# An mLSTM cell and a squared-ReLU FFN on one core: two block sums, two products and one rounding step change their places

## The chip, the cores and the metric

The kernel runs on one core of a Trainium2 chip. The metric is the device time of one execution in microseconds, as the median of several runs. A core has TensorE (PE, matmuls and their weight loads), VectorE (DVE), ScalarE (ACT), GpSimd (POOL) and SyncE (SP, whose queue issues nearly all DMAs here). Each engine takes its own instructions in the order in which they were written, and waits for the others by semaphores.

## The reference

Two layers follow each other. The first is an mLSTM cell, a recurrence over 768 steps for 4 x 8 heads of 40 elements, with a gated state; the second an FFN without bias on its 3072 output rows of 8 x 40 = 320 elements.

```python
batch, n_heads, seq, head_dim = (4, 8, 768, 40)
for t in range(S):
    m_new = np.maximum(f_gate[:, :, t] + m, i_gate[:, :, t])
    f_stab = np.exp(f_gate[:, :, t] + m - m_new)
    i_stab = np.exp(i_gate[:, :, t] - m_new)
    m = m_new
    C = f_stab[..., None, None] * C + i_stab[..., None, None] * np.einsum('bhd,bhe->bhde', vt, kt)
    n = f_stab[:, :, None] * n + i_stab[:, :, None] * kt
    h_tilde = np.einsum('bhde,bhe->bhd', C, qt)
    denom = np.maximum(np.abs(np.einsum('bhd,bhd->bh', n, qt)[:, :, None]), 1.0)
    y[:, :, t] = 1.0 / (1.0 + np.exp(-o_gate[:, :, t])) * h_tilde / denom
# rows (b, t), columns (head, d): x is 3072 x 320, w_in 320 x 2048, w_out 2048 x 320
h = np.maximum(x @ w_in, 0.0)
out = h * h @ w_out
```

The weights come as 64-bit floats and are rounded to 32 bits on the chip.

## The kernel before

**Chunks and groups.** The sequence is cut into chunks of 128 steps, six for each batch element, 24 in all (s = 0 to 23). Within a chunk the recurrence is a causal matrix of 128 x 128 for each head: the scores k q (`scores`, L415, into `tp`) are multiplied on DVE by weights W made on ACT (L384), which gives P (`weighted`, L435). From chunk to chunk the state C is handed on. Two chunks make a group of 256 rows for the FFN, 12 groups in all (g = 0 to 11).

**A chunk in its later form (s from 6 on).** `score(s)` puts the scores on PE and P on DVE, and for chunks that do not begin a sequence also the scaled query, `scale_q` (L483, written as `kq` over a buffer of that name). `attend_turned(s)` (L493) puts the numerator on PE, first from the state and the scaled query (L505), then from the values and P (L512), then the state's increment dC (L522); DVE turns the numerator (L527, `tn`) and adds up the state (L533). The numerator goes to memory and back in another order (`move_num`); `normalise_turned` (L553 to L562) makes x of it on DVE; `store_rows` sends x to memory and brings it back in squares, which `turn_squares` transposes on DVE (L597, `xT`) one chunk later. `turn_kq` (L315) is the same for k and q of a chunk to come.

**The FFN of a group.** `ffn1_main` and `ffn1_rest` (L621, L632) are x times w_in, in four parts; ACT takes the relu (L647, `r_sb`) and DVE squares it (L654) into `g2`. From group 1 on, the second product is the fast one of `ffn2_fast`: a product of 2 x 2 blocks by seven products in place of eight (each `product`, L715, is eight matmuls of eight block columns). It needs sums of blocks of the weights (T0, T1, T2, and one written over a part of `w_out`; `sums_of_weights`, L689 to L696) and of the activations (S1, S2, the third written into `g2` itself, and S4; `sums`, L710, one DVE instruction each of 128 x 1024 elements). It runs in four steps with two banks X and Y in PSUM:

- step 0: X = A11 B11, copied by ACT (L735) to `m1`; Y = S2 T1, added by DVE to `m1`
- step 1: X += A12 B21, copied to the result by ACT (L740); Y += (third sum) times B12, which DVE adds up
- step 2: a product with T2 and one with T0, each added up by DVE; the upper half of the rows goes out
- step 3: the product with S4 is added to the bank that holds the one with T0, and DVE adds it up; the other half goes out

**What sets the order.** It is written out by hand. A list `parts` holds one FFN part for each place n (1: first product, 2: second); s = 6 + n // 4 is the chunk that is worked on beside it and at = n % 4 the quarter of it. The loop at L926 puts, at each place, first what belongs to at 0, 1 or 3 (the score, the numerator, the normalising), then sums, then the FFN part, then what belongs to at 2 or to the end. From n = 8 on, step 0 of a group falls on at 0 and step 1 on at 1 of a chunk with even s, step 2 and 3 on at 2 and 3 of the next one; the first product of group g + 2 stands between. While chunks last, then, one group takes two chunks.

**Weights.** `Rounding` brings the 64-bit weights in pieces (26 in all) and turns them into 32-bit ones: two ACT instructions, three DVE instructions (L206, L210, L211) and one on GpSimd (L215) for each piece. A table, NEXT, says how many pieces are done after each place.

Of the kernel before, what the change touches and what calls it, by code (L numbers as in the profile page):

```python
# [29 lines left out]
def kernel(  # L30
# [38 lines left out]
    NPAIR = NF // 2  # L69
    GT = 2  # L70
    NG = NT // GT
# [76 lines left out]
    pieces = []  # L148
# [81 lines left out]
    rounding = Rounding()  # L230
# [452 lines left out]
    T = {}  # L683
# [36 lines left out]
    def ffn2_fast(g, step):  # L720

        if step == 0:
            st["y"] = [ffn.tile([P, DM], F32, name="y_sb", bufs=3) for _ in range(2)]
        if step in (0, 2):
            st["o2"] = [ps_h.tile([P, W], F32, name="h_ps") for _ in range(2)]
        (X, Y), (y1, y0) = st["o2"], st["y"]
        g4 = st["g2", g][:].rearrange("p (f two) t -> p f two t", two=2)
        cols = [slice(n * P, (n + 1) * P) for n in range(2)]
        S1, S2, S4 = st["S"]
        X, Y = X[:, :DH], Y[:, :DH]  # L730
        add = lambda to, a, b: nc.vector.tensor_tensor(to, a, b, op=ALU.add)  # L731
        m1, u12, u22 = y1[:, :DH], y0[:, DH:], y1[:, DH:]
        if step == 0:
            product(X, g4[:, :, 0, cols[0]], B11, start=True)
            nc.scalar.copy(m1, X)  # L735
            product(Y, S2, T[1], start=True)
            add(u12, Y, m1)
        elif step == 1:
            product(X, g4[:, :, 1, cols[0]], B21)
            nc.scalar.copy(y0[:, :DH], X)  # L740
            product(Y, g4[:, :, 0, cols[1]], B12)
            add(u22, Y, m1)
        elif step == 2:
            product(Y, g4[:, :, 1, cols[1]], T[2], start=True)
            add(m1, u22, Y)
            product(X, S1, T[0], start=True)
            add(u22, u22, X)
            t = g * GT + 1
            nc.sync.dma_start(out[t * P : (t + 1) * P, :], y1[:])
        else:  # L750
            product(X, S4, B22)
            add(u12, u12, X)
            t = g * GT
            nc.sync.dma_start(out[t * P : (t + 1) * P, :], y0[:])
# [94 lines left out]
    rounding.step()  # L849


    NEXT = (5, 8, 10, 11, 13, 15, 17, 19, 21, 23, 25, 26)
    assert NEXT[-1] == len(pieces)
    for u in range(8):
        s = 2 + u // 2
        relu_half()
# [64 lines left out]
    for g in range(1, NG):  # L921
        parts += [(2, g, i) for i in range(2)]
        if g + 2 < NG:
            parts += [(1, g + 2, i) for i in range(4)]
        parts += [(2, g, i) for i in range(2, 4)]
    for n, (which, g, i) in enumerate(parts):  # L926
        s, at = 6 + n // 4, n % 4
        if n == 1:
            decays(s + 1)
            mask(s + 1)  # L930
        if n == 4:
            brought.close()
            late = ctx.enter_context(tc.tile_pool(name="late", bufs=1, side="right"))
        if at == 0:
            do(score, s)
        if at == 1:
            do(attend_turned, s)
            if s > X_SQ:
                do(turn_squares, s - 1)
        if 5 <= n < 8:  # L940
            sums_of_weights(n - 5)
        if n == 6:
            sums(1, slice(0, NPAIR), (1, 2))
        if n == 8:
            sums_of_weights(3)
            sums(1, slice(0, NPAIR), (3,))
        if n == 9:
            sums(1, slice(0, NPAIR), (4,))
        new_sums = which == 2 and 0 < g < NG - 1 and i == 3
        if new_sums:  # L950
            for one in (1, 2, 3):
                sums(g + 1, slice(0, NPAIR), (one,))
        if at == 3:
            do(normalise_turned, s)
            do(store_rows, s)
            if s % 4 == 3:
                for r in range(s + 1, min(s + 5, NT)):
                    sigmoid(r)
        if which == 1:
            ffn1_main(g, i)  # L960
            if i % 2 == 0:
                held = st["half"]
            else:

                both = held, st["half"]
                for more, half in enumerate(both):
                    ffn1_rest(g, i - 1 + more, half[0])
                for half in both:
                    st["half"] = half
                    relu_half()  # L970
                    square_half()
        elif g == 0:
            ffn2(g, *divmod(i, 2))
        else:
            ffn2_fast(g, i)
        if new_sums:
            sums(g + 1, slice(0, NPAIR), (4,))
        if at == 2:
            do(load_squares, s + 2)
            do(weigh_on, s + 1)  # L980
            do(turn_kq, s + 1)
        if at == 3:
            do(decay_C, s + 1)
        if n < 4:
            while rounding.done < NEXT[8 + n]:
                rounding.step()
        if at == 1:
            do(move_num, s)
            do(load, s + 4)
            if 8 <= s < 20:  # L990
                load_o(s + 4)
            do(pair_up, s + 3)
# [30 lines left out]
```

## Time and profile before

| | |
|---|---|
| median of 3 runs | 565.14 us (563.45 to 567.63) |
| the profiled execution | 565.71 us, its span 563.9 us |
| PE busy | 534.4 us, 95% of the span |
| DVE busy | 333.9 us, 59% |
| ACT busy | 193.1 us, 34% |
| GpSimd busy | 95.5 us, 17% |
| mean granted PE clock | 0.976 of full speed |

A timeline row has the start in us from the span's start, the length in us, the engine, the line, the operation, the tiles written and read, the shape and the count of instructions merged; in square brackets stand the idle time of the engine before it and what ended it. PEld is the weight load of a matmul, which overlaps the one before. A matmul on 32-bit floats is two passes, so eight matmuls are 16 in a row of the timeline. The ends of matmuls are modelled, so rows of PE that follow each other closely overlap by some hundredths. The span is the time from the first to the last instruction; the execution's time is 1.8 us longer.

### The profile page before, as it was taken

The numbers are of one execution on the slowest core, as the hardware profiler recorded it, in microseconds if no ns is written. First come the engines' busy times: TensorE is split into PE (matmuls) and PEld (weight loads), VectorE is DVE, ScalarE is ACT, GpSimd is POOL, SyncE is SP. The second block draws the span as 40 slices with busy tenths as digits, with TensorE's granted clock in tenths as the row PEclk, the third lists the DMA queues.
The fourth block names the chain that finished last, engine by engine and source line by source line (L and its number), as shares of the span: only waits on it lengthen the run. The fifth ranks groups of instructions, "written<-read, shape, count | busy, mean of one in ns | idle before, by whom it ended". The sixth has DMA issues, their size and how long they took to land.

```text
span 563.9 us, 10278 instructions
## 1 busy us (share of the span) xinstructions
PE 534.4 (95%) x3928; PEld 464.6 (82%) x3929; DVE 333.9 (59%) x620; ACT 193.1 (34%) x460; POOL 95.5 (17%) x110
## 2 busy tenths in 40 slices
PE   9989899997999899999899989999989989999997
PEld 5878788876888798888888878898878878898997
DVE  8588988685945833844844655565664555341540
ACT  3767577451442221532321623321523313102100
POOL 3354623231120210010310201000200201000000
PEclk9897999998999989999989989999999989999999
DMA  9988788854665764756756736657645321110000
GB/s 194 239 181 174 155 194 210 188 117 109 143 131 118 145 132 107 154 123 127 146 107 123 145 89 136 127 134 135 137 115 112 71 65 45 48 42 1 25 23 24
DMA packets 238353, 67.53 MB, mean 120 GB/s; under 512 B 185728, under 2 KB 232832, under 8 KB 238304
## 3 DMA queue, kind: packets, MB, share of 16 engines
q1 hardware_dynamic: 238208, 66.68, 55.1%
q8 instruction: 31, 0.51, 0.4%
q10 hardware_dynamic: 96, 0.20, 0.1%
q14 instruction: 18, 0.15, 0.1%
HBM read 54.56 MB, written 17.86 MB: 128 GB/s over the span
## 4 chain that ended last, share of the span: by engine, by line
PE 83%; DVE 9%; DMA 3%; ACT 2%; issue 1%; SPq 1%; POOL 0%; DVEq 0%; POOLq 0%; ACTq 0%
PE h_ps L715 30%; PE h_ps L621 27%; PE h_ps L632 7%; PE numT L512 4%; PE tp L422 4%; PE numT L505 3%; PE h_ps L661 2%; DVE P_sb L435 2%; DVE g L654 2%; PE hp L458 1%; PE dC L522 1%; DMA num_rows<-tn 1%; DVE mag L210 1%; ACT W_sb L384 1%; PE tp L410 1%
## 5 line engine op out<-in xcount | busy, mean ns | idle before, releaser
L621 PE MATMUL h_ps<-xT,w_in 128*128 128x256 f32 x768 | 175.3, 384 | 1.2 <-ACT xT L606 0.6
L621 PEld LDWEIGHTS h_ps<-xT,w_in 128*128 128x128 f32 x768 | 143.8, 191 | 23.1 <-issue 1.2
L654 DVE TENSOR_TENSOR g<-r_sb 128x512 f32<-128x512 f32 x96 | 61.7, 701 | 76.4 <-ACT r_sb L647 76.4
L647 ACT ACTIVATE r_sb<-h_ps 128x512 f32<-128x512 f32 x96 | 49.9, 601 | 152.5 <-PE h_ps L632 149.3
L715 PE MATMUL h_ps<-w_out,g 128*128 128x160 f32 x528 | 78.4, 306 | 0.0
L715 PEld LDWEIGHTS h_ps<-w_out,g 128*128 128x128 f32 x528 | 73.9, 193 | 1.4
L358 POOL TENSOR_SCALAR_AFFINE_SELECT A_bc<-A_bc 128x1024 f32<-128x1024 f32 x22 | 25.7, 1168 | 222.3 <-ACT kq L368 128.5
L384 ACT ACTIVATE W_sb<-A_bc,b_T 128x128 f32<-128x128 f32 x176 | 53.8, 392 | 24.1 <-POOL A_bc L358 24.1
L715 PE MATMUL h_ps<-T,S 128*128 128x160 f32 x352 | 51.4, 299 | 0.0
L632 PE MATMUL h_ps<-xT,w_in 64*128 64x256 f32 x384 | 49.0, 391 | 0.0
L715 PEld LDWEIGHTS h_ps<-T,S 128*128 128x128 f32 x352 | 49.0, 190 | 0.0
L632 PEld LDWEIGHTS h_ps<-xT,w_in 64*128 64x128 f32 x384 | 34.8, 186 | 12.3 <-issue 9.0
L527 DVE STREAM_TRANSPOSE tn<-numT 128x512 f32<-128x512 f32 x18 | 12.9, 717 | 41.5 <-PE numT L512 41.5
L396 POOL TENSOR_TENSOR vw<-va,W_sb 128x328 f32<-128x328 f32 x20 | 20.1, 1006 | 86.5 <-ACT W_sb L384 69.7
L505 PE MATMUL numT<-kq,C 40*64 40x128 f32 x240 | 18.5, 299 | 15.4 <-DVE kq L483 15.4
L740 ACT COPY y_sb<-h_ps 128x160 f32<-128x160 f32 x11 | 3.2, 292 | 82.9 <-PE h_ps L715 82.9
L715 PE MATMUL h_ps<-w_out,S 128*128 128x160 f32 x176 | 26.8, 306 | 4.5 <-DVE y_sb L731 4.5
L505 PEld LDWEIGHTS numT<-kq,C 40*64 40x64 f32 x240 | 14.5, 144 | 19.8 <-issue 12.6
L435 DVE TENSOR_TENSOR P_sb<-tp,W_sb 128x512 f32<-128x512 f32 x46 | 29.5, 682 | 1.9 <-PE tp L422 1.9
L715 PEld LDWEIGHTS h_ps<-w_out,S 128*128 128x128 f32 x176 | 24.2, 190 | 7.2 <-DVE y_sb L731 7.2
L731 DVE TENSOR_TENSOR y_sb<-y_sb,h_ps 128x160 f32<-128x160 f32 x33 | 10.5, 319 | 27.6 <-PE h_ps L715 26.6
L422 PEld LDWEIGHTS tp<-kqT 40*128 40x128 f32 x384 | 24.2, 187 | 3.3 <-issue 1.3
(119 smaller groups left out, 648.6 us busy)
## 6 DMA issues: line engine op xcount, KB each, us to landing
A_bc<-a_rows SPq DMA_DIRECT2D x22, 512.0 KB, 4.8
raw<-in_moe_w_out_dram SPq DMA_DIRECT2D x16, 320.0 KB, 3.3
num_rows<-tn SPq DMA_DIRECT2D x18, 256.0 KB, 2.2
kq<-num_rows SPq DMA_DIRECT2D x72, 64.0 KB, 1.9
kqT<-kq_rows SPq DMA_DIRECT2D x34, 128.0 KB, 3.0
raw<-in_moe_w_in_dram SPq DMA_DIRECT2D x8, 512.0 KB, 4.9
kq<-in_k_dram SPq DMA_DIRECT2D x24, 160.0 KB, 3.4
va<-in_v_dram SPq DMA_DIRECT2D x24, 160.0 KB, 3.8
```

Of the source, the lines that this page charges most:

```text
L358: nc.gpsimd.affine_select(A[:], A[:], compare_op=ALU.is_ge, fill=-1e30, base=0, pattern=[[0, H], [1, P]], channel_multiplier=-1,)
L384: nc.scalar.activation(d["W"][:, i * n + h, :], A[i][:, h, :], AF.Exp, bias=b_T[:, b, c, i * n + h : i * n + h + 1],)
L396: nc.gpsimd.tensor_tensor(d["vw"][:], d["va"][:], d["W"][:, :, P - 1 : P].to_broadcast([P, H, D1]), op=ALU.mult,)
L422: nc.tensor.matmul(sc[i][:, j, :], lhsT=d["kT"][rows, j, :], rhs=d["qT"][rows, j, :], start=True, stop=True,)
L435: nc.vector.tensor_tensor(t, d["sc"][i], d["W"][:, heads, :], op=ALU.mult)
L505: nc.tensor.matmul(numT[halves[i], j, :], lhsT=C[live[i], j * D1 : j * D1 + DP], rhs=d["eA"][live[i], j, :], start=(j == 0), stop=False, s ...
L512: nc.tensor.matmul(numT[halves[i], j, :], lhsT=va_w[s % NKQ][:, h * D1 : h * D1 + DP], rhs=d["P"][h % 2][:, h // 2, :] if s < KQ_SQ else d ...
L621: nc.tensor.matmul(hs[i][:, n, :], lhsT=w_in[:, a, fb * P : (fb + 1) * P], rhs=xT[:, :, a, :], start=(n == 0 and a == 0), stop=False,)
L632: nc.tensor.matmul(hs[i][:, n, :], lhsT=w_in2[rows, 2 * pp + n, :], rhs=xT[rows, :, 2, :], start=False, stop=(n == 1),)
L647: nc.scalar.activation(rs[-1][:], h[:], AF.Relu)
L654: nc.vector.tensor_tensor(g4[:, :, i, :], r[:], r[:], op=ALU.mult)
L715: nc.tensor.matmul(to, lhsT=lhsT[:, p], rhs=rhs[:, p, :], start=(start and p == 0), stop=(p == NPAIR - 1), skip_group_check=True,)
```

## The change

Three things move; no arithmetic is added or taken away.

1. The third and fourth block sum of the activations. Before, all four of group g + 1 were queued at step 3 of group g, three ahead of the normalising and the fourth behind the step's product. Now the first two stay there, the third is queued at step 0 of group g + 1 behind `score`, and the fourth at step 1 behind `attend_turned` and `turn_squares`. Group 1 is as it was.
2. The order in `ffn2_fast`. In step 2 the product with T0 (bank X) comes ahead of the one with T2 (bank Y), and the adds of steps 1 and 2 write to other halves of `y1` accordingly.
3. The last rounding step. The table's end (now LAST) has 25 at n = 3 in place of 26, and a fifth entry, so that piece 26 is rounded at the end of n = 4, behind P of chunk 7. The pool in which T0 to T2 and the sums lie, which takes the place of the rounding's buffers, is opened at n = 5 in place of n = 4.

```diff
@@ ffn2_fast @@
             product(Y, g4[:, :, 0, cols[1]], B12)
-            add(u22, Y, m1)
+            add(m1, m1, Y)
         elif step == 2:
+            product(X, S1, T[0], start=True)
+            add(u22, m1, X)
             product(Y, g4[:, :, 1, cols[1]], T[2], start=True)
-            add(m1, u22, Y)
-            product(X, S1, T[0], start=True)
-            add(u22, u22, X)
+            add(m1, m1, Y)
             t = g * GT + 1
             nc.sync.dma_start(out[t * P : (t + 1) * P, :], y1[:])
@@ the loop over parts @@
+    LAST = (21, 23, 25, 25, 26)
     for n, (which, g, i) in enumerate(parts):
...
-        if n == 4:
+        if n == 5:
             brought.close()
             late = ctx.enter_context(tc.tile_pool(name="late", bufs=1, side="right"))
...
-        new_sums = which == 2 and 0 < g < NG - 1 and i == 3
-        if new_sums:
-            for one in (1, 2, 3):
+        if which == 2 and 0 < g < NG - 1 and i == 3:
+            for one in (1, 2):
                 sums(g + 1, slice(0, NPAIR), (one,))
+        if which == 2 and g > 1 and i < 2:
+            sums(g, slice(0, NPAIR), (3 + i,))
...
-        if new_sums:
-            sums(g + 1, slice(0, NPAIR), (4,))
...
-        if n < 4:
-            while rounding.done < NEXT[8 + n]:
+        if n < 5:
+            while rounding.done < LAST[n]:
                 rounding.step()
```

The first place is DVE's queue from step 3 of group 1 to step 1 of group 2, that is around chunk 10. S_1495 is S4 and g_1196 the activations of group 2, into which the third sum is written; x_sb and dm belong to the normalising of chunk 9, kq_89 is the scaled query of chunk 10. Before, from the middle of the normalising on:

```order
L561 TENSOR_TENSOR x_sb<-x_sb,dm 128x320
L562 COPY x_sb<-x_sb 128x64
L731 TENSOR_TENSOR y_sb<-y_sb,h_ps 128x160
L710 TENSOR_TENSOR S_1495<-g_1196,S_1494 128x1024
L435 TENSOR_TENSOR P_sb<-tp,W_sb 128x512 x2
L483 TENSOR_TENSOR kq_89<-kq_89,kqT_95 128x512
L731 TENSOR_TENSOR y_sb<-h_ps,y_sb 128x160
L527 STREAM_TRANSPOSE tn<-numT 128x4x4x32
L533 TENSOR_TENSOR C_1178<-dC,Cd 40x164 x2
L597 STREAM_TRANSPOSE xT<-xT 128x384
```

The third sum stood ahead of the normalising there. Now, from the same instruction on:

```order
L561 TENSOR_TENSOR x_sb<-x_sb,dm 128x320
L562 COPY x_sb<-x_sb 128x64
L731 TENSOR_TENSOR y_sb<-y_sb,h_ps 128x160
L435 TENSOR_TENSOR P_sb<-tp,W_sb 128x512 x2
L483 TENSOR_TENSOR kq_89<-kq_89,kqT_95 128x512
L710 TENSOR_TENSOR g_1196<-g_1196 128x8x128
L731 TENSOR_TENSOR y_sb<-h_ps,y_sb 128x160
L527 STREAM_TRANSPOSE tn<-numT 128x4x4x32
L533 TENSOR_TENSOR C_1178<-dC,Cd 40x164 x2
L597 STREAM_TRANSPOSE xT<-xT 128x384
L710 TENSOR_TENSOR S_1495<-g_1196,S_1494 128x1024
```

S4 has moved from ahead of P to behind the transpose of x, and the third sum to directly behind the scaled query.

The second place is PE's queue at steps 2 and 3 of group 1. T_1467 is T0, T_1530 is T2, S_1493 is S1 and S_1495 is S4:

```order
 L621 MATMUL h_ps<-xT,w_in 128x256 x8
 L632 MATMUL h_ps<-xT,w_in_103 128x256 x8
+L715 MATMUL h_ps<-T_1467,S_1493 128x160 x8
 L715 MATMUL h_ps<-T_1530,g_832 128x160 x8
-L715 MATMUL h_ps<-T_1467,S_1493 128x160 x8
 L715 MATMUL h_ps<-w_out,S_1495 128x160 x8
 L422 MATMUL tp<-kqT_95 128x128 x8
```

The product with T0 has moved ahead of the one with T2, which now stands between it and the product of step 3 on the same bank.

The third place is DVE's queue at n = 4 and 5, around chunk 7. mag and raw are the rounding's buffers, kq_90 is the scaled query of chunk 7:

```order
 L654 TENSOR_TENSOR g_1196<-r_sb 128x2x256 x4
-L206 TENSOR_SCALAR mag<-mag 128x320
-L210 TENSOR_SCALAR mag<-mag 128x320
-L211 SCALAR_TENSOR_TENSOR mag<-raw,mag 128x320
-L435 TENSOR_TENSOR P_sb<-tp,W_sb 128x512 x2
-L483 TENSOR_TENSOR kq_90<-kq_90,kqT_96 128x512
+L435 TENSOR_TENSOR P_sb<-tp,W_sb 128x512 x2
+L483 TENSOR_TENSOR kq_90<-kq_90,kqT_96 128x512
+L206 TENSOR_SCALAR mag<-mag 128x320
+L210 TENSOR_SCALAR mag<-mag 128x320
+L211 SCALAR_TENSOR_TENSOR mag<-raw,mag 128x320
 L527 STREAM_TRANSPOSE tn<-numT 128x4x4x32
```

The three instructions of the last rounding step have gone behind P and the scaled query of that chunk. On ACT and SP nothing moves; on GpSimd only two lines that clear the state buffers have another line number.

More of the change, by code (lines that the diff above doesn't have):

```diff
@@ L849 @@
     rounding.step()
[L852 to L853 removed]
+    NEXT = (5, 8, 10, 11, 13, 15, 17, 19)
     for u in range(8):
@@ L925 @@
         parts += [(2, g, i) for i in range(2, 4)]
+    LAST = (21, 23, 25, 25, 26)
+    assert LAST[-1] == len(pieces)
     for n, (which, g, i) in enumerate(parts):
```

## The prediction

> **What bounds the kernel now.** I read the page first, then the waits of TensorE (PE), then the timelines of VectorE (DVE) and PE around the longest of these waits, then a table by stages with the granted clock.
>
> ```profile
> span 563.9 us, 10278 instructions
> PE 534.4 (95%) x3928; PEld 464.6 (82%) x3929; DVE 333.9 (59%) x620; ACT 193.1 (34%) x460; POOL 95.5 (17%) x110
> ...
> PE numT L505 <- DVE kq L483: 15.4, 6, 4.0
> PE h_ps L715 <- DVE y_sb L731: 4.5, 11, 0.4
> PE numT L512 <- DVE P_sb L435: 0.8, 4, 0.3
> ...
> PEld h_ps L715 <- ACT r_sb L647: 3.0, 9, 0.3
> ```
>
> PE is busy for 534.4 of 563.9 us, so a change that keeps its matmuls can only win the other 29.5 us, and what PE loses by a slower clock inside its busy time. The waits (total us, times, longest) say that 20.7 us of the 29.5 are three waits for DVE: the numerator matmuls at L505 wait for the scaled query (L483) six times, the fourth step of the fast product waits for an add that reads its bank (L731) eleven times, and the numerator at L512 waits for P. The change touches exactly these three places, so I looked at the one around chunk 10 (s = 10) from both sides.
>
> ```profile
> 186.11 0.32 DVE L731 TENSOR_TENSOR y_sb<-y_sb,h_ps 128x160 f32<-128x160 f32 x1 [1.85 <-PE h_ps L715]
> 186.35 1.24 DVE L315 STREAM_TRANSPOSE kqT<-kqT 128x1024 f32<-128x1024 f32 x1
> ...
> 188.73 1.65 DVE L710 TENSOR_TENSOR S<-S,g 128x1024 f32<-128x1024 f32 x1
> 190.30 1.48 DVE L710 TENSOR_TENSOR g<-g 128x1024 f32<-128x1024 f32 x1
> 191.71 0.16 DVE L553 TENSOR_SCALAR dm<-kq 128x8 f32<-128x8 f32 x1
> ...
> 193.41 0.32 DVE L731 TENSOR_TENSOR y_sb<-y_sb,h_ps 128x160 f32<-128x160 f32 x1
> 193.63 1.22 DVE L710 TENSOR_TENSOR S<-g,S 128x1024 f32<-128x1024 f32 x1
> 194.77 1.28 DVE L435 TENSOR_TENSOR P_sb<-tp,W_sb 128x512 f32<-128x512 f32 x2
> 195.97 0.68 DVE L483 TENSOR_TENSOR kq<-kq,kqT 128x512 f32<-128x512 f32 x1
> 196.57 0.32 DVE L731 TENSOR_TENSOR y_sb<-h_ps,y_sb 128x160 f32<-128x160 f32 x1
> 199.22 0.72 DVE L527 STREAM_TRANSPOSE tn<-numT 128x512 f32<-128x512 f32 x1 [2.33 <-PE numT L512]
> ...
> 200.75 0.58 DVE L597 STREAM_TRANSPOSE xT<-xT 128x384 f32<-128x384 f32 x1 [0.27 <-issue]
> 205.40 0.33 DVE L731 TENSOR_TENSOR y_sb<-h_ps,y_sb 128x160 f32<-128x160 f32 x1 [4.08 <-PE h_ps L715]
> ...
> 186.49 2.44 PE L715 MATMUL h_ps<-w_out,S 128*128 128x160 f32 x16 [0.41 <-DVE y_sb L731]
> ...
> 192.23 2.34 PE L715 MATMUL h_ps<-T,S 128*128 128x160 f32 x16
> 196.80 1.09 PE L505 MATMUL numT<-kq,C 40*64 40x128 f32 x16 [2.23 <-DVE kq L483]
> ```
>
> From the add at 186.11 to the scaled query at 195.97 DVE runs without a pause, and PE, done with its two products at 194.57 (192.23 + 2.34), waits 2.23 us for the end of that row of work. So in this stretch DVE sets the time, and what stands in its queue ahead of L483 is on the path. The third block sum (written into g, 190.30) and the fourth (193.63) are two of those; PE needs neither before the numerator.
>
> The stretches that begin with the numerator (start:end, length, busy times, then PEclk, the granted clock) show a second loss:
>
> ```profile
> 130.20:133.60 3.40, 3.40 (x37) 3.06 (x34) 0.00 (x0) 0.00 (x0) 0.00 (x0) 0.51 0.60 173
> ...
> 196.80:205.20 8.40, 8.40 (x80) 8.14 (x81) 1.91 (x5) 1.44 (x3) 0.45 (x1) 0.80 0.40 106
> 282.98:291.33 8.35, 8.35 (x81) 7.98 (x81) 1.92 (x5) 1.44 (x3) 0.45 (x1) 0.80 0.30 82
> 328.07:336.49 8.42, 8.42 (x81) 8.02 (x82) 1.91 (x5) 1.95 (x3) 0.00 (x0) 0.80 0.32 86
> 414.05:420.85 6.80, 6.80 (x80) 6.58 (x81) 1.91 (x5) 1.94 (x3) 0.00 (x0) 1.00 0.39 106
> 457.59:466.00 8.41, 8.41 (x81) 8.02 (x81) 1.92 (x5) 1.44 (x3) 0.45 (x1) 0.80 0.33 89
> ```
>
> The last five rows are the same 80 matmul passes behind a wait at L505. Four took 8.40 us on average at a mean granted clock of 0.80, one took 6.80 at 1.00. A pause of some 2.2 us is thus followed, four times in five, by a stretch at half clock that costs 1.60 us more.
>
> **Part one: the third and fourth sums behind P and the scaled query.** Nothing is added or removed; two DVE instructions per group move. The third goes from 190.30 to behind 195.97, the fourth behind the transpose of x (200.75). From start to start they held the queue 191.71 - 190.30 = 1.41 and 194.77 - 193.63 = 1.14 us, together 2.55. PE lost 2.23 + 0.41 = 2.64 us between the same two points, so the path gains the smaller, 2.55, and a wait of about 0.1 stays. Five groups have this form (15.4 us less the 4.0 of chunk 7 is 11.4, five times about 2.3): **5 x 2.55 = 12.75 us**. The third sum's 1.48 is not in every group:
>
> ```profile
> L710 DVE TENSOR_TENSOR g<-g 128x1024 f32<-128x1024 f32 x9 | 12.3, 1363 | 0.0
> ```
>
> The mean of nine is 1.36 us; with 1.22, the fourth's length, as the short form, five of 1.48 and four of 1.22 give 12.3. Were it short everywhere, the five groups would gain 2.28 each, 1.35 us less in all: that is this term's lower end, and 2.64 each (13.2) the upper.
>
> Where they go, they have cover. The third sum stands ahead of the add at 196.57 and of the numerator's transpose, and DVE idles 2.33 us before the latter, against 1.22. PE needs its result only in the second product of step 1, after numerator and one product. The fourth stands behind the transpose of x, which waits for a DMA; queued behind it are one add of step 1 and the next chunk's kqT transpose, and DVE idles 4.08 us at that spot (205.40). It is read in step 3, two steps of FFN work later. Cost taken: nothing. If the cover went, it would be 1.2 us a group on DVE first, and on PE only beyond these pauses.
>
> **What the clock does then.** If the pauses before L505 shrink to 0.1 us, the half-clock stretches behind four of them go: **4 x 1.60 = 6.4 us**. The lower end is 0, weighed below as a rival. The 0.41 us pauses are no trigger in any row here.
>
> **Part two: the order in steps 2 and 3.** PE did the product with T2 first, then T0, and step 3 adds into T0's bank, so it waited 0.41 us for DVE to read that bank, eleven times. Now T0 comes first and T2's product (2.34 us in its like at 192.23) stands between; the add needs 0.32 us, so the wait goes. The two adds become three rewritten ones of the same shape and count (L731), none longer. Five of the eleven pauses are already in the 2.55; the other six give 2.5 us. With the wait at L512, in the groups whose chunk begins a sequence (0.8 us; P comes two sums earlier there), **3.3 us**. T0's product also goes to a bank whose relu is long past, where T2's bank was among the last to be evicted: the weight loads show 3.0 us in nine pauses for that, but PE's own waits have no such row. Bounds 0 and 3.0; I take 0, as PE is what counts.
>
> **Part three: the last rounding step behind the eighth chunk's P.**
>
> ```profile
> 126.81 0.32 DVE L206 TENSOR_SCALAR mag<-mag 128x320 f32<-128x320 f32 x1
> ...
> 128.05 1.29 DVE L435 TENSOR_TENSOR P_sb<-tp,W_sb 128x512 f32<-128x512 f32 x2
> 129.25 0.68 DVE L483 TENSOR_TENSOR kq<-kq,kqT 128x512 f32<-128x512 f32 x1
> ...
> 129.99 1.77 PE L505 MATMUL numT<-kq,C 40*64 40x128 f32 x16 [4.04 <-DVE kq L483]
> 133.96 13.19 PE L661 MATMUL h_ps<-w_out,g 128*128 128x320 f32 x48
> 138.31 1.45 DVE L689 TENSOR_TENSOR T<-w_out 128x1280 f32<-128x1280 f32 x1
> ```
>
> The three DVE instructions of the rounding step take 128.05 - 126.81 = **1.24 us** ahead of P; behind L483 they end near 130, and GpSimd's add follows. The readers of those weights come at 133.96 at the earliest (L661) and 138.31 (the weight differences, whose pool now opens one step later, still ahead of its first write). So the wait of 4.04 us becomes 2.8; that is still longer than the 2.2 of the others, and I leave the half-clock stretch at 130.20 in place (upper end: another 1.6 gone).
>
> **Sum.** 12.75 + 6.4 + 3.3 + 1.24 = 23.7 us. The profiled execution took 565.71 us (span 563.9), 0.6 over the median of the three runs shown, 565.14. 565.7 - 23.7 = **542 us**.
>
> **Rivals.**
>
> *The clock stays.* The half-clock stretches come at much the same rate whatever is done about 2.2 us pauses, because the pause is not what makes them. For: one pause of 2.23 us (before 414.05) had none. Against: every such stretch in the middle of the trace begins within 2 us of the end of a pause at L505. Time: 542.0 + 6.4 = 548.4 us. Chance 0.12. The Trainium skill, TensorE: Matmul & The Clock Gate, section "Part 1: The HAM clock gate", says that the clock halves after an idle window of about 3.4 us, which runs freely. By its letter a pause of 2.2 us could not bring it about and this rival would hold; the trace differs, since four of five such pauses were followed by one.
>
> *Another releaser close behind.* With the sums gone the numerator waits for something nearly as late: the scores, the weights W, or GpSimd's work on the same memory beside DVE. For: 1.48 against 1.22 us shows that DVE is slowed there at times. Against: between 186.11 and 195.97 no DVE row waits for another engine. If half of parts one and two and of the clock is given back (half of 22.5), about 553 us. Chance 0.10.
>
> *The trip of x takes over, and the kernel is slower.* The first FFN product of the next group needs x of the chunk before, which goes from DVE to memory and back.
>
> ```profile
> DVE xT L597 <- DMA xT<-x_rows: 22.7, 10, 3.6
> ...
> 237.43 0.20 DVE L562 COPY x_sb<-x_sb 128x64 f32<-128x64 f32 x1
> ...
> 244.79 0.58 DVE L597 STREAM_TRANSPOSE xT<-xT 128x384 f32<-128x384 f32 x1 [2.15 <-DMA xT<-x_rows]
> ...
> 246.02 7.07 PE L621 MATMUL h_ps<-xT,w_in 128*128 128x256 f32 x32
> ```
>
> The trip takes 7.4 us (237.43 to 244.79) and x is ready 0.65 us before PE takes it. After the change x leaves 1.1 to 1.4 us earlier, as the third sum stood ahead of it, and PE arrives 0.8 to 4.1 us earlier; about 1 us is left in both kinds of group (chunk 10: ready 201.33 - 1.41 = 199.9, wanted 205.20 - 4.15 = 201.05). Beyond that each us of a longer trip costs one per group, and from a pause of 2.2 us 1.6 more by the clock. To come out at 571.4 it would have to take back 23.7 and 5.7 more over eight groups, 3.7 each: 2.1 of pause and 1.6 of clock, a trip of 7.4 + 1.0 + 2.1 = 10.5 us. The transfers themselves are the same, in the same order on the same queue; only the pace rises by 4%. Chance 0.04.
>
> *No change to speak of.* That the instructions do not move is ruled out by their order as built; that everything is given back in small waits would need two causes at once. Chance 0.06.
>
> **How the numbers follow.** Forecast 0.68, the four rivals 0.12, 0.10, 0.04 and 0.06. The low end is the sum with the upper ends of the unknowns: 542 less 3.0 (relu) and 1.6 (chunk 7's clock), 537. The high end takes in the clock rival with the lower end of part one, 548.4 + 1.35, 550. Between them lie the first two cases, 0.80. About 1% (5.7 us) is what a measurement of this kernel can tell from no change: faster by more, below 559.5, holds for the forecast and two rivals, 0.90; within, 0.06; slower, 0.04.
>
> **What would show it.** In the profile after: the wait at L505 falls from 15.4 us in six to about 3 in one, plus small rests; the 4.5 us at L715 and the 0.8 at L512 are gone; the stretches from numerator to FFN product are near 6.8 us at clock 1.00; the third sum runs behind L483 and the fourth behind L597; DVE's busy time and all counts are as before. It is wrong if L505 still waits over 1 us in the middle groups, if half-clock stretches turn up without pauses, or if L621 waits for x.

## The result and the profile after

The change makes the kernel faster: 541.5 us as the median of four runs (540.11 to 544.73) against 566.23 us for the kernel before beside it, a ratio of 0.958 (95% interval 0.952 to 0.964). The forecast was 542. The profiled execution is the longest of the four, 544.73 us; against the 565.71 of the profile before that is 21.0 us less, 21.3 in the span, and the terms below are held against this 21.3.

First the page and the waits of the kernel after (total us, times, longest).

```profile
span 542.6 us, 10288 instructions
...
PE 525.0 (97%) x3929; PEld 457.9 (84%) x3929; DVE 333.0 (61%) x620; ACT 193.5 (36%) x460; POOL 97.1 (18%) x110
...
DVE xT L597 <- DMA xT<-x_rows: 46.3, 16, 4.6
...
PE numT L505 <- DVE kq L483: 6.3, 6, 2.9
...
PEld h_ps L715 <- ACT r_sb L647: 3.0, 9, 0.3
...
PE h_ps L621 <- DVE xT L597: 2.8, 3, 1.1
```

DVE has the same work as before, 333.0 us. The wait at L505 has fallen from 15.4 to 6.3 us, of which 2.9 is chunk 7 and 3.4 are rests of 0.64 to 0.85 us in five groups. The waits at L715 for the add (4.5 us) and at L512 for P (0.8) have no row any more. Two rows have grown: PE waits 2.8 us at L621 for x, where before it was 0.3, and DVE waits 46.3 us in sixteen for the return of x, where it was 22.7 in ten.

Next, the timelines of DVE, GpSimd and PE after, around chunk 10, the place that the prediction showed of before.

```profile
185.07 0.32 DVE L731 TENSOR_TENSOR y_sb<-y_sb,h_ps 128x160 f32<-128x160 f32 x1 [1.85 <-PE h_ps L715]
...
189.26 0.43 DVE L553 TENSOR_SCALAR dm<-kq 128x8 f32<-128x8 f32 x1
...
191.46 1.28 DVE L435 TENSOR_TENSOR P_sb<-tp,W_sb 128x512 f32<-128x512 f32 x2
192.66 0.68 DVE L483 TENSOR_TENSOR kq<-kq,kqT 128x512 f32<-128x512 f32 x1
193.26 1.22 DVE L710 TENSOR_TENSOR g<-g 128x1024 f32<-128x1024 f32 x1
...
200.65 0.58 DVE L597 STREAM_TRANSPOSE xT<-xT 128x384 f32<-128x384 f32 x1 [3.73 <-DMA xT<-x_rows]
201.15 1.30 DVE L710 TENSOR_TENSOR S<-g,S 128x1024 f32<-128x1024 f32 x1
...
188.22 1.44 POOL L488 TENSOR_TENSOR Cd<-C,kq 128x164 f32<-128x164 f32 x1
...
182.70 2.34 PE L715 MATMUL h_ps<-T,g 128*128 128x160 f32 x16
184.87 2.34 PE L715 MATMUL h_ps<-w_out,S 128*128 128x160 f32 x16
...
193.49 1.09 PE L505 MATMUL numT<-kq,C 40*64 40x128 f32 x16 [0.64 <-DVE kq L483]
...
201.28 3.07 PE L621 MATMUL h_ps<-xT,w_in 128*128 128x256 f32 x13 [0.83 <-DVE xT L597]
```

From the add to the start of L483 it is now 192.66 - 185.07 = 7.59 us, where it was 195.97 - 186.11 = 9.86: DVE's row of work is 2.27 us shorter. The third sum runs directly behind L483 and takes 1.22 us; the fourth has left this row for the place behind the transpose of x (201.15). At the right end is the new wait: x comes back at 200.65, and PE waits 0.83 us for it.

The table by stages (start:end, length, busy times of PE, PEld, DVE, ACT, POOL, then the granted clock) shows the clock behind the first and the last of the five numerators, and behind chunk 7's.

```profile
193.49:200.45 6.96, 6.96 (x80) 6.50 (x80) 2.47 (x5) 1.44 (x3) 0.60 (x1) 1.00 0.44 118
...
441.05:447.85 6.80, 6.80 (x81) 6.58 (x81) 4.16 (x7) 1.44 (x3) 0.45 (x1) 1.00 0.43 112
128.87:131.90 3.03, 3.03 (x49) 2.77 (x49) 1.44 (x4) 0.00 (x0) 0.86 (x1) 0.75 0.78 203
```

The same 80 matmul passes take 6.80 to 6.96 us at full clock in all five groups; four of five took about 8.40 before. In the clock's record of the whole run, before had seven stretches at half clock, after has three: two in the first 50 us, and the one behind chunk 7's pause, as before.

### The profile page after: what moved, and what is told of

The parts are those of the page before. It is cut to its first block, busy times and chain, and to the rows that moved or that the text cites. A ratio compares the mean times of both kernels' runs of the same rounds, so it can differ in the third digit from the quotient of the medians.

```text
span 542.6 us, 10288 instructions
## 1 busy us (share of the span) xinstructions
PE 525.0 (97%) x3929; PEld 457.9 (84%) x3929; DVE 333.0 (61%) x620; ACT 193.5 (36%) x460; POOL 97.1 (18%) x110
## 4 chain that ended last, share of the span: by engine, by line
PE 74%; DVE 10%; DMA 7%; SPq 4%; issue 2%; ACT 2%; POOL 0%; DVEq 0%; POOLq 0%; ACTq 0%
PE h_ps L621 26%; PE h_ps L715 25%; PE h_ps L632 7%; PE tp L422 3%; PE numT L512 3%; PE numT L505 3%; PE h_ps L661 3%; DMA x_rows<-x_sb 2%; DMA xT<-x_rows 2%; PE hp L458 1%; DVE g L654 1%; DMA num_rows<-tn 1%; SPq L308 1%; ACT W_sb L384 1%; DMA raw<-in_moe_w_out_dram 1%
## 5 line engine op out<-in xcount | busy, mean ns | idle before, releaser
L621 PE MATMUL h_ps<-xT,w_in 128*128 128x256 f32 x768 | 175.8, 384 | 3.8 <-DVE xT L597 2.8
L621 PEld LDWEIGHTS h_ps<-xT,w_in 128*128 128x128 f32 x768 | 143.7, 191 | 26.5 <-DVE xT L597 4.2
L715 PE MATMUL h_ps<-w_out,g 128*128 128x160 f32 x528 | 77.0, 302 | 0.0
L715 PEld LDWEIGHTS h_ps<-w_out,g 128*128 128x128 f32 x528 | 72.5, 190 | 1.4
L358 POOL TENSOR_SCALAR_AFFINE_SELECT A_bc<-A_bc 128x1024 f32<-128x1024 f32 x22 | 27.2, 1237 | 200.5 <-ACT kq L368 105.5
L715 PE MATMUL h_ps<-T,S 128*128 128x160 f32 x352 | 52.3, 302 | 0.0
L715 PEld LDWEIGHTS h_ps<-T,S 128*128 128x128 f32 x352 | 48.8, 190 | 3.0 <-ACT r_sb L647 3.0
L597 DVE STREAM_TRANSPOSE xT<-xT 128x384 f32<-128x384 f32 x18 | 10.4, 576 | 46.3 <-DMA xT<-x_rows 46.3
L396 POOL TENSOR_TENSOR vw<-va,W_sb 128x328 f32<-128x328 f32 x20 | 20.1, 1003 | 86.6 <-ACT W_sb L384 74.9
L731 DVE TENSOR_TENSOR y_sb<-y_sb,h_ps 128x160 f32<-128x160 f32 x44 | 14.1, 320 | 33.8 <-PE h_ps L715 32.6
L422 PE MATMUL tp<-kqT 40*128 40x128 f32 x384 | 26.9, 279 | 0.0
L715 PE MATMUL h_ps<-T,g 128*128 128x160 f32 x176 | 25.7, 299 | 0.0
L715 PE MATMUL h_ps<-w_out,S 128*128 128x160 f32 x176 | 25.7, 299 | 0.0
```

The source lines that it names most:

```text
L358: nc.gpsimd.affine_select(A[:], A[:], compare_op=ALU.is_ge, fill=-1e30, base=0, pattern=[[0, H], [1, P]], channel_multiplier=-1,)
L396: nc.gpsimd.tensor_tensor(d["vw"][:], d["va"][:], d["W"][:, :, P - 1 : P].to_broadcast([P, H, D1]), op=ALU.mult,)
L422: nc.tensor.matmul(sc[i][:, j, :], lhsT=d["kT"][rows, j, :], rhs=d["qT"][rows, j, :], start=True, stop=True,)
L621: nc.tensor.matmul(hs[i][:, n, :], lhsT=w_in[:, a, fb * P : (fb + 1) * P], rhs=xT[:, :, a, :], start=(n == 0 and a == 0), stop=False,)
L715: nc.tensor.matmul(to, lhsT=lhsT[:, p], rhs=rhs[:, p, :], start=(start and p == 0), stop=(p == NPAIR - 1), skip_group_check=True,)
```

## The experiments

Two questions were open when the result stood: whether the clock's 6.4 us really came from the pauses and not from the other edits, and what each part is worth by itself. A third came with the profile after: whether the new wait for x is what holds the kernel now. The first four kernels ran on one chip (565.75 us for the kernel before there), the next four on a second (567.15), the last four on a third (564.73).

### Only the sums moved

Before, with part one of the change.

```diff
-            for one in (1, 2, 3):
+            for one in (1, 2):
                 sums(g + 1, slice(0, NPAIR), (one,))
+        if which == 2 and g > 1 and i < 2:
+            sums(g, slice(0, NPAIR), (3 + i,))
...
-            sums(g + 1, slice(0, NPAIR), (4,))
```

> The first part alone: third and fourth sum behind P and the scaled query; order of steps 2 and 3 and rounding as before. Theory (DVE's queue ahead of L483 sets the numerator, and a pause of 2.2 us brings a half-clock stretch of 1.6 us): the five pauses at L505 of 2.2 us fall to under 0.2 us, as step 3's own pause stays in front of them; no half-clock stretch after 135 us; 5 x 2.27 + 4 x 1.6 + 0.8 = 18.5 us less, about 547 us beside a profile of 565.7. Rival (the clock has nothing to do with the pauses): 12.2 us less, about 553.5, with half-clock stretches still in the middle of the trace.

Measured: 550.55 us, ratio 0.975 (0.970 to 0.981), 15.2 us less than before. Its waits:

```profile
PE h_ps L715 <- DVE y_sb L731: 4.5, 11, 0.4
...
PE numT L505 <- DVE kq L483: 4.4, 2, 4.2
...
PE h_ps L621 <- DVE xT L597: 3.7, 3, 1.6
```

Without the other order of the products, PE arrives later and the middle groups have almost no wait left at L505: 4.4 us, of which 4.2 is chunk 7. There is no half-clock stretch in the middle of this trace. Of the 3.3 us that are missing to what was expected, the last row can account for most: 3.7 us for x, where it was 0.3. The account is not closed, though: the half clock behind chunk 7 lasts twice as long here (6.83 us), and the first 50 us have none, where before had two stretches.

### Only the order of the products

Before, with part two.

```diff
-            add(u22, Y, m1)
+            add(m1, m1, Y)
         elif step == 2:
+            product(X, S1, T[0], start=True)
+            add(u22, m1, X)
             product(Y, g4[:, :, 1, cols[1]], T[2], start=True)
-            add(m1, u22, Y)
-            product(X, S1, T[0], start=True)
-            add(u22, u22, X)
+            add(m1, m1, Y)
```

> The second part alone: T0's product ahead of T2's in step 2. Theory: the eleven pauses of 0.41 us at step 3 go, but in the five groups where DVE's queue decides, PE only waits the longer at L505 (2.2 grows to about 2.8 us), so only six of them count: some 3 us less, about 562 us, half-clock stretches as many as before or one more. Rival (the parts add up independently): eleven count, about 6 us less, 559.5.

Measured: 567.52 us, ratio 1.004 (1.001 to 1.007), no gain but a loss of 1.8 us. Its waits, one numerator, and of the five stretches behind the numerators the two longest and the sum:

```profile
PE numT L505 <- DVE kq L483: 19.0, 6, 4.2
PE numT L512 <- DVE P_sb L435: 2.2, 4, 0.9
...
PE h_ps L621 <- DVE xT L597: 2.0, 2, 1.1
...
197.64 1.97 PE L505 MATMUL numT<-kq,C 40*64 40x128 f32 x16 [2.92 <-DVE kq L483]
...
197.64:207.26 9.62, 9.62 (x80) 9.19 (x81) 1.92 (x5) 1.45 (x3) 0.44 (x1) 0.69 0.36 95
...
329.91:339.93 10.02, 10.02 (x80) 9.59 (x81) 1.92 (x5) 1.94 (x3) 0.00 (x0) 0.66 0.36 93
...
sum 44.85, PE 44.84 PEld 42.92 DVE 9.58 ACT 8.22 POOL 1.39; mean PE 8.97 PEld 8.58 DVE 1.92 ACT 1.64 POOL 0.28
```

The eleven pauses at L715 are gone, as they should be. But where DVE's queue sets the time, PE only arrives earlier and waits longer: 2.92 us instead of 2.23. All five pauses are now followed by half clock, two of them by one twice as long (the stretches of 9.62 and 10.02 us). Together the five stretches take 44.85 us; before they took 40.38. That 4.5 us, the 1.4 more at L512 and the 1.7 more at L621 are more than the pauses won. With the first part in place it is another matter: the ratio to the kernel before goes from 0.975 to 0.958 with parts two and three, or to 0.967 on another chip (below).

### Only the rounding step

Before, with part three.

```diff
+    LAST = (21, 23, 25, 25, 26)
-        if n == 4:
+        if n == 5:
...
-        if n < 4:
-            while rounding.done < NEXT[8 + n]:
+        if n < 5:
+            while rounding.done < LAST[n]:
```

> The third part alone: last rounding step behind chunk 7's P. Theory: the wait of 4.0 us at L505 near 126 us falls to about 2.9, a half-clock stretch still follows it, 1.1 to 1.2 us less, which the timing can hardly tell from no change. Rival (GpSimd's part of the rounding, now later, holds up L661 or the weight differences): L661 or L689 wait, nothing gained.

Measured: 563.77 us, ratio 0.997 (0.993 to 1.000), 2.0 us less, an interval that reaches to no change. Chunk 7's pause fell from 4.04 to 3.3 us, and the whole wait at L505 from 15.4 to 14.6. The half clock that was expected behind chunk 7's pause did not come; one came at 148 us instead, behind a pause of 1.4 us. Of the five pauses of 2.2 to 2.4 us in the middle groups, which this kernel leaves as they were, three were followed by half clock here, not four.

Alone, then, the parts give 15.2, -1.8 and 2.0, together 15.4 us; all three at once gave 24.7. They ran on different chips. The interval of the first part alone (0.970 to 0.981) does not touch that of the whole change in the first comparison (0.952 to 0.964), but it touches that of the whole change on the third chip (0.963 to 0.971, 18.3 us). That the three together give more than their sum is likely, then, but not shown.

### The pauses filled with matmuls of zeros

Before, unchanged but for nine matmuls of zeros ahead of the numerator in the five groups with a pause. They go into the numerator's bank, which the numerator then overwrites. PE waits no less for DVE; it is only not idle. The inserted lines shift the numbers: the numerator is L512 here, the FFN product L628.

```diff
+    FILL = {10: 9, 14: 9, 16: 9, 20: 9, 22: 9}
...
+        for _ in range(FILL.get(s, 0)):
+            nc.tensor.matmul(
+                numT[:].rearrange("p j t -> p (j t)"), lhsT=zeros[:, :1].to_broadcast([P, P]),
+                rhs=zeros[:, :1].to_broadcast([P, W]), start=True, stop=True, skip_group_check=True,
+            )
```

> The kernel before, with nine matmuls on zeros (128x512, bf16, into the numerator's own bank, which the numerator overwrites) ahead of L505 in chunks 10, 14, 16, 20 and 22, so that PE works through about 2 of the 2.2 us for which it waits. No wait is taken away. Theory (an idle PE is what brings the half clock): the half-clock stretches in the middle go and the numerator stretches take 6.8 in place of 8.4 us: 4 x 1.6 = 6.4 us less, about 559.5. Rival (half clock comes at that rate anyway, or work on zeros is no activity to it): 565.7 and 8.4 us as before.

Measured: 559.15 us, ratio 0.990 (0.984 to 0.995), 6.6 us less. PE's timeline around chunk 10, and the wait that is left:

```profile
194.11 1.91 PE L503 MATMUL numT<-zeros 128*128 128x512 bf16 x8
...
196.29 1.09 PE L512 MATMUL numT<-kq,C 40*64 40x128 f32 x16 [0.27 <-DVE kq L484]
...
203.10 1.24 PE L628 MATMUL h_ps<-xT,w_in 128*128 128x256 f32 x5
...
PE numT L512 <- DVE kq L484: 5.6, 6, 4.0
```

(The row counts eight of the nine matmuls.) From numerator to FFN product it is 203.10 - 196.29 = 6.81 us, where it was 8.40; after the half clock at chunk 7, which was not filled, there is none to the end of the work. Work that computes nothing, put into the pause, brings 6.6 us, with an interval of 3.0 to 8.8, where 6.4 was forecast. This settles that the idle pause makes the clock fall, and that the clock's term is of the size forecast.

### The fourth sum put back

After, with the fourth sum once more ahead of P. This sizes one sum by itself and makes pauses between those of before and after.

```diff
-        if which == 2 and g > 1 and i < 2:
-            sums(g, slice(0, NPAIR), (3 + i,))
+        if which == 2 and g > 1 and i == 0:
+            sums(g, slice(0, NPAIR), (3,))
...
+        if new_sums:
+            sums(g + 1, slice(0, NPAIR), (4,))
```

> The changed kernel with the fourth sum put back ahead of P (behind step 3's product, as before); the third stays moved. It puts 1.14 us back into DVE's queue ahead of L483. Theory (that queue decides): the five pauses at L505 grow from 0.64 to about 1.8 us, 5.7 us more; x is waited for less, as PE comes later, 1 to 2.8 us less; about 545 to 546 beside 541.5. It also asks which pause the clock answers to: 0.85 us brought no half clock, 2.2 us did four times in five, 2.9 us always and sometimes for 6.8 us. If 1.8 us brings it, up to five times 1.6 us are added, 553. Rival (numerator bound by something else): under 543.

Measured: 553.49 us, ratio 0.976 (0.970 to 0.981). One numerator, and stretches behind numerators:

```profile
405.97 1.09 PE L505 MATMUL numT<-kq,C 40*64 40x128 f32 x16 [1.78 <-DVE kq L483]
...
195.26:202.06 6.80, 6.80 (x80) 6.58 (x81) 3.06 (x6) 1.44 (x3) 0.44 (x1) 1.00 0.39 100
...
405.97:414.37 8.40, 8.40 (x80) 8.14 (x81) 3.06 (x6) 1.94 (x3) 0.00 (x0) 0.80 0.38 103
450.20:458.60 8.40, 8.40 (x81) 8.14 (x82) 3.04 (x6) 1.44 (x3) 0.45 (x1) 0.80 0.39 102
```

The pause is 1.78 us instead of 0.64: the fourth sum costs 1.14 us a group, just what was read from start to start. Two of the five pauses brought half clock. 5 x 1.14 and 2 x 1.60 make 8.9 of the 10.8 us by which its span (553.4) is longer than that of after; the other 1.9 stay open, and the two ran on different chips.

### What holds the kernel now: the trip of x, and what stands ahead of it

In the profile after, x leaves DVE earlier and yet takes longer. SyncE's queue around the store of chunk 11's x, first of before, then of after:

```profile
234.87 0.51 SPq L333 DMA_DIRECT2D A_bc<-a_rows  x1
...
237.66 0.38 SPq L588 DMA_DIRECT2D x_rows<-x_sb  x1
240.00 2.75 SPq L590 DMA_DIRECT2D xT<-x_rows  x4
```

```profile
231.69 0.78 SPq L333 DMA_DIRECT2D A_bc<-a_rows  x1
232.70 0.58 SPq L588 DMA_DIRECT2D x_rows<-x_sb  x1
237.38 1.86 SPq L590 DMA_DIRECT2D xT<-x_rows  x4
```

The loads that bring x back are issued as soon as the store of x has landed, so the store's time is the gap ahead of L590: 240.00 - 237.66 = 2.34 us before, 237.38 - 232.70 = 4.68 after. Before, a load of 512 KB (A_bc, for weights of later chunks) was issued 2.8 us ahead of the store; now it is 1.0 us ahead, and the store lands 0.7 us after that load has. The Trainium skill, DMA: Bandwidth & Descriptors, section "Queues, rings and completion order", says that a DMA engine takes the descriptors of one ring in order; the trace agrees with that, by the 0.7 us.

Chunk 11 shows this at its largest. In the profile after, all fifteen stores of x up to 415 us landed 0.5 to 0.7 us behind the load ahead of them. For the even chunks 10 to 20 the change did little: the load stood mostly 0.6 to 0.8 us ahead already, and the store took 4.2 to 4.8 us before and 4.2 to 4.4 after. For the six odd chunks 9 to 19 the load was 1.7 to 3.8 us ahead and the store took 2.4 us on average; now it is 1.0 to 2.2 us ahead, and the store takes 4.0. Not every wait for x is this, however: for the x that PE waits for around chunk 10 (0.83 us, shown above) the store took 3.5 us both before and after. There the last of the four loads that bring x back landed after 4.3 us, where it was 2.2; why, no run here shows.

Four kernels changed this trip or what leads to it. The first puts the load behind the store, the second shortens DVE's queue ahead of L483 once more (the first sum goes into step 2, between its adds), the third does both.

```diff
@@ weigh_on @@
-        do(load_A, s + 2)
@@ the loop over parts @@
             do(store_rows, s)
+            do(load_A, s + 3)
```

```diff
             add(u22, m1, X)
+            if g < NG - 1:
+                sums(g + 1, slice(0, NPAIR), (1,))
             product(Y, g4[:, :, 1, cols[1]], T[2], start=True)
...
-            for one in (1, 2):
+            for one in (2,):
```

> The changed kernel with the load of a chunk's A_bc (512 KB) issued behind the store and the reloads of x in place of just ahead of them. Theory (the store of x lands half a us after A_bc does, so it waits behind that load in the DMA rings): the store takes about 2.1 us from issue to landing in place of 3.6 to 4.7, and PE's wait for x at L621 (2.8 us in three) falls under 0.5 us: about 539. Rival (the trip is long by itself): store and wait as they were, 541.5. It may cost at the numerator's trip, which then meets the load: DVE's wait for kq (L553) would grow.

> The changed kernel with the first sum (S1) queued in step 2, between its two adds, where DVE idles 1.85 us for PE. Theory (DVE's queue still decides by 0.64 us): the rest at L505 goes; but PE then comes to L621 earlier and x does not, so much of the 5 x 0.64 = 3.2 us returns there: 539 to 541, with L621 waiting 4 to 6 us in all. Rival (the rest at L505 is a fixed cost of the semaphore): 541.5 with 0.64 us still there.

> Both of the last two: A_bc's load behind x's trip and S1 in step 2. Theory: neither L505 nor L621 waits to speak of, 2.8 + 3.2 = 6 us less than the changed kernel, about 535.5. Rival (a third thing stands right behind, such as the numerator's trip or P's own products): 538 or more, with a new row in PE's waits.

Measured, as ratios to the kernel before beside them: 545.83 us, 0.964 (0.958 to 0.970); 544.81 us, 0.964 (0.956 to 0.971); 545.35 us, 0.962 (0.957 to 0.966). None is better than after (0.958, 0.952 to 0.964). Where each gain went can be read. The load behind the store, in the DMA view (KB each, median us from issue to landing, 140 to 430 us) and the waits:

```profile
num_rows<-tn SPq DMA_DIRECT2D x14, 256.0 KB, 4.6
x_rows<-x_sb SPq DMA_DIRECT2D x14, 192.0 KB, 2.8
...
DVE dm L553 <- DMA kq<-num_rows: 28.3, 9, 4.7
...
PE h_ps L621 <- DVE xT L597: 4.9, 3, 2.4
```

The store of x takes 2.8 us at the median, in place of 4.3 after, as expected, but the wait at L621 did not fall with it (4.9 us against 2.8). Now the store of the numerator stands behind the load, 4.6 us in place of 2.3, and DVE waits 28.3 us at L553 for it, where it was 10.9. The cost was handed on, not saved.

With the first sum moved, the rests at L505 are gone, and PE waits for x instead:

```profile
PE h_ps L621 <- DVE xT L597: 8.1, 6, 2.3
...
PE numT L505 <- DVE kq L483: 3.1, 1, 3.1
```

8.1 us at L621 against 2.8 after, 3.1 at L505 against 6.3: most of one went into the other. With both edits, two pauses at L621 of 2.8 and 3.1 us were followed by half clock as well.

So the load must stand close ahead of neither store. The fourth kernel issues it later still, behind `pair_up` at at = 1 of the next chunk, which puts it some 5 to 6 us ahead of the next store of x; it ran on a third chip, together with the changed kernel itself.

```diff
@@ weigh_on @@
-        do(load_A, s + 2)
@@ the loop over parts @@
             do(pair_up, s + 3)
+            if s > X_SQ:
+                do(load_A, s + 2)
```

> The changed kernel once more, as it is, on the chip and in the call of the last three, to compare them with. Expected: 0.957 of the kernel before, 541 to 543 us.

> The changed kernel with A_bc's load issued a quarter of a chunk after its buffer comes free, behind the loads of k and q of the next chunk, some 4 us ahead of the store of x in place of 1 to 2. Theory (the store waits behind that load, and nothing else was near): the store takes 2.1 to 3 us in place of 3.6 to 4.7, PE's wait for x at L621 falls from 2.8 us to under 0.5, and DVE's wait for the numerator's trip (L553) stays near 11 us; some 2.5 us less than the changed kernel of this call. Rival (the DMA engines are simply full there, and what one trip wins another loses): no difference.

The changed kernel took 546.48 us on this chip (544.94 to 547.05), ratio 0.967 (0.963 to 0.971); the one with the later load 543.59 us (541.99 to 544.22), ratio 0.962 (0.958 to 0.966), 2.9 us less. The runs of the two, four each, do not overlap; the intervals of their ratios do. Its DMA view, and then its wait at L505 and L621, with the changed kernel's wait at L621 on the same chip behind it:

```profile
x_rows<-x_sb SPq DMA_DIRECT2D x14, 192.0 KB, 2.7
...
PE numT L505 <- DVE kq L483: 7.0, 7, 3.0
...
PE h_ps L621 <- DVE xT L597: 1.4, 1, 1.4
```

```profile
PE h_ps L621 <- DVE xT L597: 6.1, 5, 2.6
```

The store takes 2.7 us, the numerator's is as it was (2.4), and the wait for x falls from 6.1 to 1.4 us. The same changed kernel waited 2.8 us for x in the first comparison and 6.1 on this chip. That is 3.3 us of the 5.0 between its two medians, 541.5 and 546.5; the rest is not accounted for.

The last two kernels fill chunk 7's pause with twelve matmuls of zeros (overwritten, as above): one is after with that alone, the other the kernel with the later load, the first sum in step 2 and the fill.

```diff
+    FILL = {7: 12}
```

> The changed kernel with twelve matmuls on zeros (into the numerator's bank) in PE's wait of 2.9 us before chunk 7's numerator. Theory (an idle PE brings the half clock): the half-clock stretch near 130 us goes, the stretch from that numerator on is 1.6 us shorter, 1.6 us less than the changed kernel of this call. Rival: no difference.

> The last one together with S1 in step 2 and twelve matmuls on zeros in PE's wait before chunk 7's numerator. Theory: no wait at L505 but chunk 7's, none at L621, no half clock near 130 us: 2.5 + 3.2 + 1.6 = 7 us less than the changed kernel of this call. Rival (x's trip still ends last): L621 waits 4 us or more and 2 us are gained at most.

Filling alone: 546.54 us, ratio 0.969 (0.963 to 0.974), nothing gained over the 546.48 of after. The half clock behind chunk 7 is gone, though, and the stretch there is about 1.1 us shorter (from the part before the numerator to the next scores 23.5 against 24.7 us). But PE then waits 5.6 us for x in four pauses, and one of these, of 2.8 us, brought a half clock at 365 us that after did not have there. All together: 542.25 us (541.23 to 545.99), ratio 0.961 (0.956 to 0.966), 4.2 us less than after on the same chip, where about 7 was expected.

```profile
PE h_ps L628 <- DVE xT L604: 5.8, 5, 2.6
```

The wait for x is back at 5.8 us: whatever is won on DVE ahead of the numerator, PE then waits for x. It is the shortest median on that chip, and below the kernel before (564.73) and the changed one (546.48) there; but its runs overlap with those of the later load alone, and one of them (545.99) with those of the changed kernel. So the later load, with no overlap, is the only one of these steps that stands out as a gain.

## Why the prediction was right, point by point

**Direction, size and the place.** The 20.7 us of waits for DVE and the clock were where the time came from. With the sums behind P the row of work on DVE sets the time less, and every wait named has fallen or gone. One of the three signs of being wrong did come: L621 waits for x.

**Part one** was forecast at 5 x 2.55 = 12.75 us, with 2.28 a group as the lower end. It came to 2.27 a group on average, 11.4. The step that failed is the price of the third sum, 1.41 us from start to start. The fourth was right to the hundredth (1.14, by the kernel with the fourth sum put back); the third was worth 2.27 - 1.14 = 1.13. Before, its first part ran beside GpSimd's L488 and took 1.48 us; after, it takes 1.22 elsewhere, but L488 now runs beside L553, which takes 0.43 us in place of 0.16, in four of the five groups. The 0.27 stayed in the queue under another line.

**The clock** was forecast at 4 x 1.60 = 6.4 us, and all four stretches are gone. They took 33.6 us together and take 27.4 now, 6.2 less. That the pause is the cause was an inference from four of five; the kernel with zeros shows it, and so the first rival (548.4 us) falls. The Trainium skill, TensorE: Matmul & The Clock Gate, section "Part 1: The HAM clock gate", gives about 3.4 us of idleness for it; the runs differ, with half clock behind pauses of 1.78 us.

**Part two** was forecast at 0.41 for each of six pauses plus 0.8, 3.3 us. The pause that the trace names is 0.41, but the time from the third product's start to the fourth's was 186.49 - 183.74 = 2.75 us before and 184.87 - 182.70 = 2.17 after, 0.58 less. The fourth product itself, up to the start of the next scores, took 188.86 - 186.49 = 2.37 us behind the pause and takes 187.14 - 184.87 = 2.27 now. That makes 0.68 each, six times 4.1, and 4.9 with the wait at L512: the term was mis-sized. The same shortfall is why a rest of 0.64 us is left at L505 where 0.1 was forecast: PE lost 2.23 + 0.68 = 2.91 between the two points, not 2.64, and DVE gave 2.27. The relu was taken at nothing, and its row at L715 is unchanged (3.0 us in nine). What neither the prediction nor the expectation of the run with this part alone (3 us less) saw is that alone it costs time.

**Part three** was forecast at 1.24 us and gave 4.04 - 2.91 = 1.1, by the pauses at L505. The half clock behind it stayed, as taken.

**The trip of x** was the rival with 0.04. It did not turn the sign, but its mechanism is there: 2.8 us at L621 where before it was 0.3. The step that failed is "about 1 us is left", which took the trip as constant at 7.4 us because the transfers are the same in the same order. From DVE's last step of x (191.12) to the transpose (200.65) it is 9.5 us in the group of chunk 10, by a slow load back; for the x of chunk 11 the store alone takes 2.3 us more. The order on the queue is the same, but the distance between the load and the store is not.

The sum of what was found: 11.4 + 6.2 + 4.9 + 1.1 - 2.5 = 21.1 us, of 21.3 in the span. The forecast of 23.7 was 2.4 above the profiled gain; it fits the medians (24.7) better than the profile it was made for, and on the third chip the gain was 18.3. So the match of 542 with the median of 541.5 is in part luck: the third sum and x took back 3.9 us, part two gave 1.6 more, and the two measurements of the change, on two chips, differ by more than either. How much of the trip's lengthening depends on the chip is left open.

**What decides whether a pause brings half clock.** By its length alone there is no rule. Two of five were followed by half clock at about 1.8 to 2.0 us (fourth sum put back), four of five at 2.2 to 2.5 (before), three of five at the same length (rounding step alone), five of five at 2.9 (order of the products alone); pauses of 1.8 to 2.6 us at L621 brought none in four of the kernels. The clock's record shows more. Within each profile all half-clock stretches start whole multiples of 3.41 us apart and last 3.41 or 6.83 us, as if the clock were set anew only at the edges of windows of that length. Two of these windows in before, each with the one behind it (length, then busy times as in the table above):

```profile
324.80:328.21 3.41, 1.18 (x11) 0.97 (x11) 3.35 (x6) 0.00 (x0) 0.00 (x0) 1.00 0.29 77
328.21:331.62 3.41, 3.41 (x32) 3.07 (x32) 0.00 (x0) 0.00 (x0) 0.00 (x0) 0.50 0.42 93
410.13:413.54 3.41, 1.68 (x13) 1.44 (x11) 3.38 (x7) 0.00 (x0) 0.00 (x0) 1.00 0.49 147
413.54:416.95 3.41, 2.90 (x52) 2.71 (x53) 1.33 (x4) 0.00 (x0) 0.00 (x0) 1.00 0.50 106
```

The pause that ended at 328.07 lies whole in one window, which leaves PE 1.18 us of work, and half clock follows. The equally long one that ended at 414.05, the one of five without half clock, is cut by a window's edge into 1.73 and 0.50 us. Over all fourteen profiles, from 100 to 500 us, half clock followed each of the 22 windows with more than 2.0 us of idle PE, 6 of the 15 with 1.6 to 2.0 us, and one with less (1.33 us). So the four of five were in part where the pauses happened to fall, and the clock's term is a matter of odds for any one execution. What decides between 1.6 and 2.0 us, and when a stretch lasts 6.83 us, stays open.

## What to carry to other kernels

Where one engine's queue sets the time of a stage, an edit that lets another engine arrive there earlier wins nothing and can lose: the pause grows, and TensorE's clock pays for it. Shorten the queue first, then price the rest on the profile that results. And before counting on a transfer that "stays the same", look at which larger one was issued just ahead of it, because moving a small store nearer to a large load on its queue is enough to take back part of the gain.

## What was not expected of the hardware

- A pause of TensorE of 1.78 us can be followed by 3.4 us at half clock, and one of about 2.9 us by double that, in two of five cases (stretches of 9.62 and 10.02 us in place of 6.80). A single one cost about 1.60 us here, and matmuls of zeros prevented it. Pauses of 2.56 and 2.58 us that a window's edge cut in two had none behind them.
- A store of 192 KB landed 2.3 us after its issue when a load of 512 KB stood 2.8 us ahead of it on the queue, and after 4.7 us when the load stood 1.0 us ahead: 0.5 and 0.7 us behind the load's own landing.
- What DVE loses beside GpSimd's L488 falls on whatever runs there: 0.26 us on a block sum before, 0.27 us on an instruction of 128x8 after. Beside GpSimd's L396 the first block sum lost nothing (1.18 us with it and without).
- The pause that the trace prints before a matmul can be less than the time lost: 0.41 us printed, 0.58 from start to start, and 0.10 more in the product behind it.
